# Attention's transfers on SyncE in program order, V in three buffers and asked for sooner, fills and a reciprocal moved later

## The chip, the cores and the metric

The kernel runs on one core of one Trainium2 chip. The metric is the device time of one execution in microseconds (us). A core has five engines that run their own instruction lists in order and wait for each other by semaphores: TensorE (PE, matmuls), VectorE (DVE), ScalarE (ACT), GpSimd (POOL) and SyncE (SP). SP computes nothing here; it issues nearly all of the transfers from memory. ACT and POOL issue a few.

## The reference, cut to what matters

Three layers follow each other. Only the first is touched by the change.

```python
# attention: q, k, v are (2, 12, 448, 64)
scores = cap * tanh(scale * q @ k.T / cap)
attn = exp(scores - max); attn = attn / (sum(attn) + 1e-9)
x = attn @ v                                   # -> (2, 448, 768)
# gated MLP with a spatial gate (w_in, g_ln, w_sg, b_sg, w_out)
h = gelu(x @ w_in); u, v = halves of h
x = x + (u * (w_sg @ layernorm(v) + b_sg)) @ w_out
# gated convolution (w_in, conv_w, w_out)
h = relu(x @ w2_in); out = (h * sigmoid(conv3(h))) @ w2_out
```

## The kernel before

**Attention.** The 24 heads are taken as 12 pairs N. A pair has two rounds R = 2N and 2N + 1 (`half` 0 and 1). In a round PE computes scores (tile `sc`), ACT takes tanh and then exp of them (`raw`, one tanh and one exp for each round), and PE multiplies the `raw` of two rounds earlier with V and with ones (tile `pv`, function `values`). So values of pair N run in rounds 2N + 2 and 2N + 3 (the first pair sooner). There is one PSUM buffer for the scores. In an even round DVE adds two halves of `raw` (`sm`), which a later multiplication with ones sums up.

After a pair's second values ACT copies `pv` to `E`; the next pair's values wait for that copy. For two pairs at a time POOL sends the sums (`ss`) through memory: `s1` in `norm` takes the reciprocal on DVE and writes it out, `s1b` reads it back to all partitions (`rb`), and `s2` multiplies `E` by `rb` on DVE and splits the result into `X`, high part on ACT and low part on DVE. `later(k, fn)` runs a step k ticks later; a round has two ticks, one between scores and values, and one behind the values.

**Fills.** The table `FILL` puts matmuls of the next layer (`mo<-X,WI`) between a round's scores and its values: in three rounds six matmuls each of the first output tile, in two later rounds 18 each of the second and third. They need `X` of finished pairs and pieces of `w_in`. Their PSUM tile `mo` has one buffer, which is free when a gelu in three steps (`g` on ACT, `g` on DVE and ACT, `u` on DVE) has read it.

**Transfers.** `load(n)` asks for q and k of pair n (`qr` with three buffers, `kr` with two), two pairs ahead. `load_v(n)` asks for three quarters of V; the fourth, for all pairs, is `vlast`. `wdec` asks for a piece of `w_in` (`f`, 512 KB, four buffers) in the rounds of `WIN`; ACT or DVE decode it in steps (`hd`, `f`, `WI`). `columns` asks for `g_ln` and `conv_w` in round 1, whose decode steps are 24 columns wide. A scheduler places the instructions of each engine by a simulated timeline of its own; `pin` (`issue_after`) keeps an instruction behind another. SP's transfers carry no pin, so that their order on SP is the scheduler's.

At the start 18 matmuls on the tile `wz` warm PE up while the first q and k come.

**Behind attention** PE runs the other layers' matmuls with no gap to speak of; the change does not alter that part's instructions.

Of the kernel before, what the change touches and what calls it, by code (L numbers as in the profile page):

```python
# [9 lines left out]
F32 = mybir.dt.float32  # L10
F32R = mybir.dt.float32r
U32 = mybir.dt.uint32
U16 = mybir.dt.uint16
# [6 lines left out]
P = 128  # L20
# [13 lines left out]

NFAST = 1

FILL = {13: (0, 0, 2), 17: (0, 2, 4), 21: (0, 4, 6), 23: (1, 0, 6), 25: (2, 0, 6)}

TAKEN = 3

# [11 lines left out]
def stages(  # L52
# [18 lines left out]
    V, A, T, G = nc.vector, nc.scalar, nc.tensor, nc.gpsimd  # L71

    now = [0]
    lasta, lastv, lastr = [None], [None], [None]

    def pin(last):
        return tc.issue_after(last[0].ins) if last[0] is not None else ExitStack()

    due = {}

    def later(k, fn):
        due.setdefault(now[0] + k, []).append(fn)
# [43 lines left out]
    def decode_half(hi, lo, src, pool, bufs, wait, hi_eng, top_eng):  # L126

        n = src.shape[1]
        r = pool.tile([P, 512, 2], U32, tag="f64", name="f64", bufs=bufs)[:, :n]
        words = r.rearrange("p c w -> p (c w)").bitcast(U16)  # L130
        nc.sync.dma_start(words[:, : 4 * n - 1], src.rearrange("r c w -> r (c w)").bitcast(U16)[:, 1:])
        low = r[:, :, 0]
        top = words.rearrange("p (c w) -> p c w", w=4)[:, :, 2].bitcast(BF16)
        heads.append(heads.pop(0))
        hd = heads[-1][:, :n]

        def s1():
            half = hd.bitcast(F16).rearrange("p (c w) -> p c w", w=2)[:, :, 1]
            with pin(lasta), pin(lastv):
                if top_eng == "a":  # L140
                    A.activation(half, top, AF.Copy)
                else:
                    V.tensor_copy(half, top)

        def s2():
            V.scalar_tensor_tensor(
                out=low, in0=low, scalar=13, in1=hd, op0=ALU.logical_shift_right, op1=ALU.bitwise_or
            )
            if hi_eng == "a":
                A.activation(hi, f(low), AF.Copy)  # L150
            else:
                V.tensor_copy(hi, f(low))

        def s3():
            V.tensor_tensor(out=lo, in0=f(low), in1=f(hi), op=ALU.subtract)

        for k, fn in zip(wait, (s1, s2, s3)):
            later(k, fn)

    def decode(hi, lo, src, pool, bufs, wait=(1, 2, 3), hi_eng="a", cols=512, low_eng="v", top_eng="a"):  # L160

        if heads:
            return decode_half(hi, lo, src, pool, bufs, wait, hi_eng, top_eng)
        n = src.shape[1]
        r = pool.tile([P, cols, 2], U32, tag="f64", name="f64", bufs=bufs)[:, :n]
        nc.sync.dma_start(r, src)
        h, l = r[:, :, 1], r[:, :, 0]

        def s1():
            with pin(lasta), pin(lastv):  # L170
                A.activation(f(h), f(h), AF.Copy, scale=2.0**-112)  # L171
                if low_eng == "a":

                    A.activation(l, l, AF.Copy, scale=0.93 * 2.0**-29)  # L174
                else:
                    V.tensor_scalar(
                        out=l, in0=l, scalar1=29, scalar2=None, op0=ALU.logical_shift_right
                    )

        def s2():  # L180
            V.scalar_tensor_tensor(  # L181
                out=l, in0=h, scalar=3, in1=l, op0=ALU.logical_shift_left, op1=ALU.bitwise_or
            )
            V.scalar_tensor_tensor(  # L184
                out=l, in0=h, scalar=0x80000000, in1=l, op0=ALU.bitwise_and, op1=ALU.bitwise_or
            )
            if hi_eng == "a":
                A.activation(hi, f(l), AF.Copy)
            else:
                V.tensor_copy(hi, f(l))  # L190

        def s3():
            V.tensor_tensor(out=lo, in0=f(l), in1=f(hi), op=ALU.subtract)

        for k, fn in zip(wait, (s1, s2, s3)):
            later(k, fn)
# [60 lines left out]
        return eye  # L257

    def columns(pool):
        nc.sync.dma_start(gbc, g_ln.partition_broadcast(P))  # L260
        decode(cw[:, 0], cw[:, 1], conv_w, pool, 4 if bounded else 3)

    def attention(att, psa):
# [10 lines left out]
        def load(n):  # L274
            b, p = divmod(n, NPAIR)
            qr = att.tile([P, S], F32, tag="qr", name="qr", bufs=3)
            kr = kraw[n % 2]
            for h in range(2):
                r = slice(h * D, (h + 1) * D)
                nc.sync.dma_start(qr[r], qT[b, p, r, h])  # L280

            dma = (nc.sync if n else nc.scalar).dma_start
            dma(kr[:D], kT[b, p, :D, 0])
            dma(kr[D:, :ST], kT[b, p, D:, 1, D:])
            dma(kr[D:, ST:], kT[b, p, D:, 1, :D])
            qraw[n] = qr, kr
# [1 line left out]
        vf = {}  # L288

        def load_v(n):  # L290
            vf[n] = att.tile([P, 3, P], F32, tag="V", name="V", bufs=2)
            nc.sync.dma_start(vf[n], vL[divmod(n, NPAIR)][:, :3])

        Qt = {}

# [28 lines left out]
        load_v(0)  # L324
        vlast = att.tile([P, B * NPAIR, P], F32, name="vlast")

        def load_vlast(eng, n0, n1):
            v = vL.rearrange("b n p g c -> p (b n) g c")
            for h in range(2):
                r = slice(h * D, (h + 1) * D)  # L330
                for c in range(2):
                    eng.dma_start(vlast[c * D : (c + 1) * D, n0:n1, r], v[r, n0:n1, 3, r])

        load_vlast(nc.scalar, 0, 3)
        if WARM:

            wz = att.tile([P, S], F32R, name="wz")
            V.memset(f(wz), 0.0)
            wps = psa.tile([P, 4, 512], F32, tag="sc", name="wps", bufs=1)[:, 0, :S]
            for i in range(WARM):  # L340
                T.matmul(wps, lhsT=wz[:, :P], rhs=wz, start=True, stop=True)  # L341
# [140 lines left out]
        def norm(N, both):  # L482
            b, p = divmod(N, NPAIR)
            if N >= B * NPAIR - NFAST:
                return norm_pe(N, both)

            j = N % 2
            last = N == B * NPAIR - NFAST - 1
            m = 1 if last else 2
            if j == 0:  # L490
                pairs[:] = (
                    att.tile([P, 2 * (S + HS)], F32, tag="E", name="E", bufs=3),
                    att.tile([P, 14], F32, tag="ss", name="ss", bufs=2)[:, : 7 * m],
                )
            e, ss = pairs
            A.activation(e[:, j * (S + HS) : (j + 1) * (S + HS)], both, AF.Copy)
            u = j * (2 * S + HS)
            G.dma_start(ss[j * P // m : (j + 1) * P // m], e[::32, u : u + HS])
            if j == 0 and not last:
                return  # L500

            rb = att.tile([P, 2, S], F32, tag="rb", name="rb", bufs=2)
            eb = e[:, HS : HS + m * S].rearrange("p (j c) -> p j c", j=m)
            rb = rb[:, :m]

            ds = []


            def s1():
                with pin(lastv):  # L510
                    V.tensor_scalar(out=ss, in0=ss, scalar1=guard, scalar2=None, op0=ALU.add)
                V.reciprocal(out=ss, in_=ss)
                ds.append(dr.tile([m, 2, 2, HS], F32, tag=f"d{m}", name="d"))
                d = ds[0]
                G.dma_start(d.rearrange("j h f (p c) -> (j h f p) c", c=7 * m), ss)

            def s1b():
                (d,) = ds
                for h in range(2):
                    for i in range(m):  # L520
                        G.dma_start(
                            rb[h * D : (h + 1) * D, i].rearrange("p (f c) -> p f c", f=2),
                            d[i, h].partition_broadcast(D),
                        )

            def s2():
                with pin(lastv):
                    V.tensor_tensor(out=eb, in0=eb, in1=rb, op=ALU.mult)
                with pin(lasta):
                    lastv[0] = split(eb, X[:, 0, p - j : p + 1, b], X[:, 1, p - j : p + 1, b], "a")  # L530

            later(3, s1)
            later(4, s1b)
            later(13, s2)

        def norm_pe(N, both):
# [20 lines left out]
        for R in range(2 * NN + LAGS[1]):  # L557
# [1 line left out]
            if R == 1:  # L559
                columns(att)  # L560
            if R == 4:
                load_vlast(nc.sync, 3, NN)
            for j, at in enumerate(WIN):
                if at == R:
                    top_eng = "v" if R < 11 else "a"
# [1 line left out]
            if R < 2 * NN:  # L567
                if half == 0 and N + 2 < NN:
                    load(N + 2)
                if R == 1:  # L570

                    start_values(0)
# [18 lines left out]
            if R - done >= LAGS[R >= LAGS[2]]:  # L591
                values(*divmod(done, 2))
                done += 1
            if half and N + 1 < NN:
                load_v(N + 1)
            tick()
        for _ in range(9):
            tick()
        assert not due
        heads.clear()  # L600
        lasta[0] = lastv[0] = None

    def exact_attention(att, psa):

# [405 lines left out]
```

## Time and profile before

| what | value |
|---|---|
| median of 3 runs | 350.54 us (350.42 to 351.92) |
| the profiled execution | 351.55 us, its span 349.8 us |
| PE busy | 322.5 us, 92% of the span |
| DVE busy | 239.3 us, 68% |
| ACT busy | 223.8 us, 64% |
| attention | the first 136 us, about |

The span runs from the first to the last instruction of the execution; the time of a run has some 1.75 us around it. Engine shares are means over stages that differ, so the stages are read one by one.

### The profile page before, as it was taken

The numbers are of one execution on the slowest core, as the hardware profiler recorded it, in microseconds if no ns is written. First come the engines' busy times: TensorE is split into PE (matmuls) and PEld (weight loads), VectorE is DVE, ScalarE is ACT, GpSimd is POOL, SyncE is SP. The second block draws the span as 40 slices with busy tenths as digits, with TensorE's granted clock in tenths as the row PEclk, the third lists the DMA queues.
The fourth block names the chain that finished last, engine by engine and source line by source line (L and its number), as shares of the span: only waits on it lengthen the run. The fifth ranks groups of instructions, "written<-read, shape, count | busy, mean of one in ns | idle before, by whom it ended". The sixth has DMA issues, their size and how long they took to land.

```text
span 349.8 us, 6271 instructions
## 1 busy us (share of the span) xinstructions
PE 322.5 (92%) x2380; PEld 263.9 (75%) x2380; DVE 239.3 (68%) x471; ACT 223.8 (64%) x357; POOL 37.7 (11%) x74
## 2 busy tenths in 40 slices
PE   8989289796979899999999999999999999999992
PEld 6456156464645678898889999999999999999992
DVE  4453847628494559999799778999795999990000
ACT  1899629769696835766676555454875789882110
POOL 4000302113130332022111100000000000000000
PEclk9999879989998999999999999999999999999999
DMA  5777665537240113421232357000286022012211
GB/s 139 212 197 238 170 176 161 140 98 197 93 136 25 57 53 118 105 84 44 64 104 74 133 165 278 0 2 0 61 252 231 5 87 88 2 52 110 80 52 34
DMA packets 22062, 37.73 MB, mean 108 GB/s; under 512 B 7320, under 2 KB 14376, under 8 KB 22024
## 3 DMA queue, kind: packets, MB, share of 16 engines
q1 hardware_dynamic: 19320, 34.21, 32.0%
q0 software_dynamic: 1632, 2.61, 2.9%
q10 hardware_dynamic: 1072, 0.43, 0.5%
q8 instruction: 20, 0.33, 0.4%
q14 instruction: 18, 0.15, 0.1%
HBM read 34.40 MB, written 2.79 MB: 106 GB/s over the span
## 4 chain that ended last, share of the span: by engine, by line
PE 79%; ACT 6%; DMA 5%; DVE 4%; SPq 3%; issue 2%; DVEq 0%; ACTq 0%
PE mo L101 17%; PE mo L102 17%; PE mo L103 17%; PE pv L365 8%; PE sc L365 4%; PE mo L365 3%; PE mo L715 3%; PE mo L716 3%; PE mo L717 3%; DMA qr<-in_qT_dram 2%; ACT raw L379 2%; PE wps L341 2%; DMA V<-in_vL_dram 2%; ACT raw L380 2%; DMA kr<-in_kT_dram 1%
## 5 line engine op out<-in xcount | busy, mean ns | idle before, releaser
L101 PE MATMUL mo<-X,WI 128*128 128x448 f32 x126 | 46.1, 367 | 0.3 <-DVE u L220 0.3
L102 PE MATMUL mo<-X,WI 128*128 128x448 f32 x126 | 46.0, 366 | 0.0
L103 PE MATMUL mo<-X,WI 128*128 128x448 f32 x126 | 45.9, 365 | 0.0
L365 PE MATMUL pv<-raw,V 128*32 128x224 f32 x576 | 36.0, 381 | 10.0 <-DMA V<-in_vL_dram 7.9
L379 ACT ACTIVATE raw<-sc 128x1792 f32<-128x1792 f32 (+1 forms) x22 | 32.4, 1471 | 12.8 <-PE sc L365 12.6
L365 PEld LDWEIGHTS pv<-raw,V 128*32 128x32 f32 x576 | 19.7, 115 | 23.5 <-issue 14.6
L380 ACT ACTIVATE raw<-raw 128x1792 f32<-128x1792 f32 (+3 forms) x26 | 36.8, 1413 | 0.8
L102 PE MATMUL mo<-HG,W 128*128 128x448 f32 x96 | 34.8, 365 | 0.0
L103 PE MATMUL mo<-HG,W 128*128 128x448 f32 x96 | 34.7, 365 | 0.0
L101 PE MATMUL mo<-HG,W 128*128 128x448 f32 x96 | 34.1, 365 | 0.0
L365 PE MATMUL sc<-Q,K 64*128 64x448 f32 x216 | 28.7, 387 | 2.3 <-ACT raw L379 2.1
L171 ACT ACTIVATE f<-f 128x256 f32<-128x256 f32 (+2 forms) x44 | 22.7, 516 | 10.3 <-DMA f<-in_w_in_dram 5.9
L365 PEld LDWEIGHTS sc<-Q,K 64*128 64x128 f32 x216 | 18.5, 185 | 12.7 <-ACT raw L379 7.2
L181 DVE SCALAR_TENSOR_TENSOR f<-f 128x256 uint32<-128x256 uint32 (+2 forms) x44 | 22.3, 516 | 8.1 <-ACT f L174 7.9
L101 PEld LDWEIGHTS mo<-X,WI 128*128 128x128 f32 x126 | 23.6, 187 | 2.8 <-DVE u L220 0.8
L102 PEld LDWEIGHTS mo<-X,WI 128*128 128x128 f32 x126 | 23.7, 188 | 2.0
L103 PEld LDWEIGHTS mo<-X,WI 128*128 128x128 f32 x126 | 23.6, 188 | 2.0
L174 ACT ACTIVATE f<-f 128x256 uint32<-128x256 uint32 (+2 forms) x44 | 22.6, 513 | 0.0
L184 DVE SCALAR_TENSOR_TENSOR f<-f 128x256 uint32<-128x256 uint32 (+2 forms) x44 | 22.4, 515 | 0.1
L895 ACT ACTIVATE o<-mo 128x448 f32<-128x448 f32 x12 | 6.3, 540 | 24.9 <-PE mo L103 21.3
L428 DVE TENSOR_TENSOR sm<-raw 128x896 f32<-128x896 f32 x12 | 13.0, 1085 | 11.1 <-ACT raw L380 9.7
L365 PE MATMUL mo<-X,WI 128*128 128x448 f32 x54 | 13.4, 388 | 6.8 <-DVE X L98 4.1
(148 smaller groups left out, 700.8 us busy)
## 6 DMA issues: line engine op xcount, KB each, us to landing
f<-in_w_in_dram SPq DMA_DIRECT2D x12, 512.0 KB, 5.7
f<-in_w_out_dram SPq DMA_DIRECT2D x24, 256.0 KB, 4.6
f<-in_w_in_dram SPq DMA_DIRECT2D x12, 511.8 KB, 4.6
f<-in_w_out_dram SPq DMA_DIRECT2D x8, 384.0 KB, 3.1
qr<-in_qT_dram SPq DMA_DIRECT2D x24, 112.0 KB, 3.0
out_dram<-o SPq DMA_DIRECT2D x12, 224.0 KB, 1.9
rb<-d POOLq DMA_DIRECT2D x22, 112.0 KB, 3.6
V<-in_vL_dram SPq DMA_DIRECT2D x12, 192.0 KB, 3.0
```

The costliest lines, as they stand in the source:

```text
L101: matmul(ps, lhsT=whi, rhs=xhi, start=start, stop=False)
L102: matmul(ps, lhsT=whi, rhs=xlo, start=False, stop=False)
L103: matmul(ps, lhsT=wlo, rhs=xhi, start=False, stop=stop)
L171: A.activation(f(h), f(h), AF.Copy, scale=2.0**-112)
L174: A.activation(l, l, AF.Copy, scale=0.93 * 2.0**-29)
L181: V.scalar_tensor_tensor(out=l, in0=h, scalar=3, in1=l, op0=ALU.logical_shift_left, op1=ALU.bitwise_or)
L184: V.scalar_tensor_tensor(out=l, in0=h, scalar=0x80000000, in1=l, op0=ALU.bitwise_and, op1=ALU.bitwise_or)
L365: lastm[0] = T.matmul(*args, **kw)
L379: A.activation(x, ps, AF.Tanh, **sc)
L380: lasta[0] = A.activation(x, x, AF.Exp, scale=creg)
L428: V.tensor_tensor(out=held[N], in0=raw[:, 0:2], in1=raw[:, 2:4], op=ALU.add)
L715: T.matmul(ps, lhsT=xs(0, k), rhs=WI[1][:, 0, k], start=k == 0, stop=False)
```

## The change

Six things change, all in attention: every transfer that SP issues there goes through `sync`, which pins it behind the one before, so SP keeps the program's order; `V` has three buffers instead of two; `load_v(N + 1)` moves from the end of round 2N + 1 to round 2N, behind `load(N + 2)`; the first part of `vlast` moves from ACT's queue to SP's; `s1` and `s1b` of `norm` come one tick later; and the three small fills move from rounds 13, 17 and 21 to 14, 18 and 22. The warm-up tile `wz` takes a buffer of the tag `rb`.

```diff
-FILL = {13: (0, 0, 2), 17: (0, 2, 4), 21: (0, 4, 6), 23: (1, 0, 6), 25: (2, 0, 6)}
+FILL = {14: (0, 0, 2), 18: (0, 2, 4), 22: (0, 4, 6), 23: (1, 0, 6), 25: (2, 0, 6)}
...
+    def sync(dst, src):
+
+        if lasts:
+            with pin(lasts):
+                lasts[0] = nc.sync.dma_start(dst, src)
+        else:
+            nc.sync.dma_start(dst, src)
...
-        nc.sync.dma_start(r, src)
+        sync(r, src)
...
-                nc.sync.dma_start(qr[r], qT[b, p, r, h])
-
-            dma = (nc.sync if n else nc.scalar).dma_start
+                sync(qr[r], qT[b, p, r, h])
+
+            dma = sync if n else nc.scalar.dma_start
...
-            vf[n] = att.tile([P, 3, P], F32, tag="V", name="V", bufs=2)
-            nc.sync.dma_start(vf[n], vL[divmod(n, NPAIR)][:, :3])
+            vf[n] = att.tile([P, 3, P], F32, tag="V", name="V", bufs=3)
+            sync(vf[n], vL[divmod(n, NPAIR)][:, :3])
...
-        load_vlast(nc.scalar, 0, 3)
+        load_vlast(0, 3)
...
-            wz = att.tile([P, S], F32R, name="wz")
+            wz = att.tile([P, S], F32R, tag="rb", name="wz", bufs=2)
...
-            later(3, s1)
-            later(4, s1b)
+            later(4, s1)
+            later(5, s1b)
             later(13, s2)
...
                 if half == 0 and N + 2 < NN:
                     load(N + 2)
+                if half == 0 and N + 1 < NN:
+                    load_v(N + 1)
...
-            if half and N + 1 < NN:
-                load_v(N + 1)
```

How it moves instructions, at three places. On SP before, from k of pair 5 on (a number behind a name tells one buffer's use from another; `V_421` is V of pair 3, `qr_424` and the `kr0` around it are q and k of pair 6, `kr1` is k of odd pairs):

```order
L283 DMA kr1_90<-in_kT_dram 64x448
L284 DMA kr1_90<-in_kT_dram 64x384
L285 DMA kr1_90<-in_kT_dram 64x64
L939 TENSOR_LOAD one_72
L939 ISA x2
L131 DMA f64_722<-in_w_in_dram 128x2047
L284 DMA kr0_89<-in_kT_dram 64x384
L280 DMA qr_424<-in_qT_dram 64x448 x2
L283 DMA kr0_89<-in_kT_dram 64x448
L285 DMA kr0_89<-in_kT_dram 64x64
L131 DMA f64_827<-in_w_in_dram 128x2047
L292 DMA V_421<-in_vL_dram 128x384
```

On SP in the changed kernel, where V of pair 3 is `V_335` and `qr_329` and `kr0` ahead of it are q and k of pair 4:

```order
L83 DMA V_256<-in_vL_dram 128x384
L83 DMA f64_309<-in_w_in_dram 128x2047
L83 DMA vlast_108<-in_vL_dram 64x9x64 x4
L83 DMA qr_329<-in_qT_dram 64x448 x2
L83 DMA kr0_89<-in_kT_dram 64x448
L83 DMA kr0_89<-in_kT_dram 64x384
L83 DMA kr0_89<-in_kT_dram 64x64
L83 DMA V_335<-in_vL_dram 128x384
L83 DMA f64_382<-in_w_in_dram 128x2047
L83 DMA qr_424<-in_qT_dram 64x448 x2
L83 DMA kr1_90<-in_kT_dram 64x448
```

V of pair 3 stood behind the loads of pairs 5 and 6 and now stands behind those of pair 4, with one piece of w_in between its round's loads and the next.

On PE before, in round 13 (its scores, the first fill, its values):

```order
L365 MATMUL sc<-Q,K_87 128x2x224 x6
L365 MATMUL sc<-qr,kl_91 64x224 x4
L365 MATMUL mo<-X,WI_76 128x448 x6
L365 MATMUL pv<-raw,vlast 64x224 x4
L365 MATMUL pv<-raw,V 32x224 x8
```

And on PE in the changed kernel, in round 14 (its scores, the first fill, its values, the scores of round 15):

```order
L373 MATMUL sc<-Q,K_88 128x448 x12
L373 MATMUL mo<-X,WI_76 128x448 x6
L373 MATMUL pv<-raw,V 32x224 x16
L373 MATMUL pv<-sm,ones_152 32x224 x4
L373 MATMUL sc<-Q,K_88 128x2x224 x6
```

The six matmuls on `mo` moved from behind round 13's scores to behind round 14's; the two other small fills moved in the same way.

On ACT before, around the gelu of the first output tile (fill done in round 21; `g_1219` is that gelu, 1792 columns of `raw` are an even round, 1344 an odd one):

```order
L379 ACTIVATE raw<-sc 128x1344
L380 ACTIVATE raw<-raw 128x1344
L213 ACTIVATE g_1219<-mo 128x448
L217 ACTIVATE g_1219<-g_1219 128x448
L141 ACTIVATE hd_141<-f_1145 128x512
L496 ACTIVATE E<-pv 128x672
L379 ACTIVATE raw<-sc 128x1792
L380 ACTIVATE raw<-raw 128x1792
```

And on ACT in the changed kernel, where the fill is done in round 22 and `g_1265` is that gelu:

```order
L149 ACTIVATE hd_141<-f_1141 128x512
L504 ACTIVATE E<-pv 128x672
L387 ACTIVATE raw<-sc 128x1792
L221 ACTIVATE g_1265<-mo 128x448
L388 ACTIVATE raw<-raw 128x1792
L225 ACTIVATE g_1265<-g_1265 128x448
L149 ACTIVATE hd_141<-f_1199 128x512
L387 ACTIVATE raw<-sc 128x1344
```

The exp of the round now stands between the gelu's two steps on ACT.

## Rows read from the trace of the kernel before

**Rows 1.** Busy time by stretch (attention, the rest); columns named in the first line.

```profile
core 0: us, PE busy (x) PEld busy (x) DVE busy (x) ACT busy (x) POOL busy (x), PEclk, DMA share, GB/s
0.00:136.00 136.00, 115.12 (x1376) 75.50 (x1377) 78.43 (x154) 95.15 (x88) 27.17 (x61) 0.95 0.50 142
136.00:350.00 214.00, 207.40 (x1006) 188.40 (x1004) 160.92 (x318) 128.66 (x269) 10.53 (x14) 1.00 0.27 86
```

**Rows 2.** PE's waits, first 140 us: us in total, times, longest.

```profile
PE pv L365 <- DMA V<-in_vL_dram: 7.9, 1, 7.9
```

**Rows 3.** Timeline of PE, 35 to 60 us: start, us, operation, [idle before <-releaser].

```profile
35.97 1.48 PE L365 MATMUL sc<-Q,K 64*128 64x448 f32 x12
45.32 3.08 PE L365 MATMUL pv<-raw,V 128*32 128x224 f32 x32 [7.87 <-DMA V<-in_vL_dram]
...
48.71 0.88 PE L365 MATMUL sc<-Q,K 64*128 64x448 f32 x6
...
52.11 1.49 PE L365 MATMUL sc<-Q,K 64*128 64x448 f32 x12
53.53 1.76 PE L365 MATMUL pv<-raw,V 128*32 128x224 f32 x32
...
55.59 0.88 PE L365 MATMUL sc<-Q,K 64*128 64x448 f32 x6
...
56.83 0.56 PE L365 MATMUL pv<-raw,vlast 64*64 64x224 f32 x8
...
58.99 1.50 PE L365 MATMUL sc<-Q,K 64*128 64x448 f32 x12
```

**Rows 4.** Busy time and granted clock (PEclk), 46 to 48 us, columns as in rows 1.

```profile
46.00:48.00 2.00, 2.00 (x28) 1.27 (x24) 0.00 (x0) 0.00 (x0) 0.00 (x0) 0.50 1.10 253
```

**Rows 5.** Timeline of SP's queue, first 40 us.

```profile
11.05 0.42 SPq L131 DMA_DIRECT2D f<-in_conv_w_dram  x1
...
17.50 2.70 SPq L332 DMA_DIRECT2D vlast<-in_vL_dram  x4
...
34.58 0.48 SPq L284 DMA_DIRECT2D kr<-in_kT_dram  x1
```

**Rows 6.** The chain that ended last, 0 to 60 us: start, us, what.

```profile
39.07 6.12 DMA V<-in_vL_dram
```

**Rows 7.** Timeline of PE, 63 to 123 us.

```profile
63.30 0.61 PE L365 MATMUL sc<-qr,kl 64*64 64x224 f32 x8
...
66.94 1.28 PE L365 MATMUL mo<-X,WI 128*128 128x448 f32 x5 [1.65 <-DVE X L98]
68.15 0.65 PE L365 MATMUL pv<-raw,vlast 64*64 64x224 f32 x8
...
71.89 1.53 PE L365 MATMUL sc<-Q,K 64*128 64x448 f32 x12
...
115.12 3.93 PE L365 MATMUL mo<-X,WI 128*128 128x448 f32 x18
...
122.23 1.76 PE L365 MATMUL pv<-raw,V 128*32 128x224 f32 x32 [0.97 <-ACT E L496]
```

**Rows 8.** Timeline of ACT, 15 to 89 us.

```profile
15.91 0.21 ACT L141 ACTIVATE hd<-f 128x24 f16<-128x24 bf16 x1
...
79.45 0.77 ACT L141 ACTIVATE hd<-f 128x512 f16<-128x512 bf16 x1
80.09 0.69 ACT L496 ACTIVATE E<-pv 128x672 f32<-128x672 f32 x1
...
83.98 0.93 ACT L97 ACTIVATE X<-E 128x896 fp32r<-128x896 f32 x1
...
86.75 1.33 ACT L380 ACTIVATE raw<-raw 128x1344 f32<-128x1344 f32 x1
```

**Rows 9.** DMA issues: tensor, queue, operation, count, KB each, median us to landing.

```profile
kr<-in_kT_dram SPq DMA_DIRECT2D x11, 16.0 KB, 2.9
```

**Rows 10.** Timeline of all engines, 106 to 110 us.

```profile
106.94 0.55 ACT L213 ACTIVATE g<-mo 128x448 f32<-128x448 f32 x1 [0.43 <-PE mo L365]
...
108.78 0.62 DVE L220 SCALAR_TENSOR_TENSOR u<-g,mo 128x448 f32<-128x448 f32 x1 [0.64 <-ACT g L217]
```

More of the change, by code (lines that the diff above doesn't have):

```diff
@@ L73, in stages @@
     now = [0]
-    lasta, lastv, lastr = [None], [None], [None]
+    lasta, lastv, lastr, lasts = [None], [None], [None], [None]
     def pin(last):
         return tc.issue_after(last[0].ins) if last[0] is not None else ExitStack()
+    def sync(dst, src):
[4 more added lines that the diff above has]
+            nc.sync.dma_start(dst, src)
     due = {}
@@ L130, in decode_half @@
         words = r.rearrange("p c w -> p (c w)").bitcast(U16)
-        nc.sync.dma_start(words[:, : 4 * n - 1], src.rearrange("r c w -> r (c w)").bitcast(U16)[:, 1:])
+        sync(words[:, : 4 * n - 1], src.rearrange("r c w -> r (c w)").bitcast(U16)[:, 1:])
         low = r[:, :, 0]
@@ L259, in columns @@
     def columns(pool):
-        nc.sync.dma_start(gbc, g_ln.partition_broadcast(P))
+        sync(gbc, g_ln.partition_broadcast(P))
         decode(cw[:, 0], cw[:, 1], conv_w, pool, 4 if bounded else 3)
@@ L325, in attention, with load_vlast @@
         vlast = att.tile([P, B * NPAIR, P], F32, name="vlast")
-        def load_vlast(eng, n0, n1):
+        def load_vlast(n0, n1):
             v = vL.rearrange("b n p g c -> p (b n) g c")
@@ L331, in load_vlast @@
                 for c in range(2):
-                    eng.dma_start(vlast[c * D : (c + 1) * D, n0:n1, r], v[r, n0:n1, 3, r])
-        load_vlast(nc.scalar, 0, 3)
+                    sync(vlast[c * D : (c + 1) * D, n0:n1, r], v[r, n0:n1, 3, r])
+        load_vlast(0, 3)
         if WARM:
-            wz = att.tile([P, S], F32R, name="wz")
+            wz = att.tile([P, S], F32R, tag="rb", name="wz", bufs=2)
             V.memset(f(wz), 0.0)
@@ L561, in attention @@
             if R == 4:
-                load_vlast(nc.sync, 3, NN)
+                load_vlast(3, NN)
             for j, at in enumerate(WIN):
@@ L601, in attention @@
         lasta[0] = lastv[0] = None
+        lasts.clear()
     def exact_attention(att, psa):
```

## The prediction

> **What bounds the kernel now.** I read the busy table by stretch first. From 136 us to the end TensorE (PE) is busy 207.4 of 214 us, and its list of waits holds nothing there; before 136 us it is busy only 115.1 of 136 [rows 1]. All that can be won lies in the attention stage. The list of PE's waits there [rows 2] gives the largest, 7.9 us for one V tile; the next are for X, the finished pairs, ahead of the fills. What these cost is read from PE's timeline, start to start, since a wait also empties the pipeline and can lower the clock.
>
> An undisturbed pair of heads is the yardstick: scores of pair 5 start at 52.11, of pair 6 at 58.99, so a pair takes 6.88 us; in it the first scores take 53.53 - 52.11 = 1.42, then values and the second scores 56.83 - 53.53 = 3.30 [rows 3].
>
> *The V stall.* Scores of pair 4 start at 35.97 and the values behind them at 45.32 instead of 37.39: 7.93 us lost. These values then run to 48.71, 3.39 us where the same piece takes 55.59 - 53.53 = 2.06: 1.33 more, because the granted clock is at half (0.50 over 46 to 48 us, 1.2 instead of 2.4 GHz) after the idle time [rows 3, 4]. Together **9.26 us**. Why V was late: the queue of SyncE (SP) issued a piece of kr only at 34.58 [rows 5], and the chain shows V asked for at 39.07 and landed 6.12 later [rows 6]. By SP's order this V, of pair 3, stands behind q and k of pair 6 and behind two pieces of w_in.
>
> *The fill stalls.* The six matmuls of a fill in round 13 begin after the scores at 63.30; the next values start at 68.15, and the next scores at 71.89 [rows 7]. From 58.99 to the values at 122.23 (less their own wait of 0.97) there are 62.27 us. Work in it: six pairs, 41.28; the large fill of 18, 3.93; three fills of six, a third of that each, 3.93; together 49.14. So **13.13 us** are lost around the three small fills and the waits on ScalarE (ACT) beside them. In the first, the values from 68.15 to 71.89 take 3.74 us where the same piece takes 58.99 - 56.83 = 2.16, the sign of the lower clock again.
>
> **The change, part by part.**
>
> *V sooner, SP in program order.* V of pair 3 is now requested in round 4 (scores of pair 2), behind one w_in piece instead of behind the loads of pair 6. With three buffers it needs only the values of pair 0, long done. It is used in round 8, so the request leads by two pairs, 13.8 us less the queue's own issues; the landing of V that stalled was 6.12 [rows 6]. For the later pairs V waits for values that end in the round just before the request; again nearly two pairs of lead. I count the whole 9.26 as gained. Queued behind V on SP are one w_in piece and the next q and k: they are asked for a round or more ahead of their use and are not due at once (priced as a rival below). The part of vlast that leaves ACT's queue gives ACT nothing: its first tanh waits for PE's first scores, and these for the warm-up.
>
> *Cost at the start.* The four vlast requests now stand on SP ahead of q and k of pair 2, then V of pair 1, and only then conv_w. Four vlast requests took 2.70 us [rows 5], so conv_w, issued at 11.05, moves to about 13.8, or 14.3 with half a microsecond for V. Its decode on ACT stands right ahead of the tanh of round 2, and ran at 15.91 without a wait [rows 8], so conv_w takes at most 15.91 - 11.47 = 4.4 us to land. At the nearest small transfer, 2.9 us for 16 KB of kr [rows 9], it lands at 14.3 + 0.4 + 2.9 = 17.6. K of pair 2 moves as well, and VectorE (DVE) prepares it ahead of conv_w's second step. The gaps in which SP waited ahead of 11.05 take up part of the shift; with half a microsecond of it there, the tanh starts 1.2 us late. ACT's chain of tanh and exp then sets round 4's scores, so this is lost for good. Bounds: 0 (the gaps take up all) and 17.6 - 15.91 + 1.5 = 3.2 (the longest landing). I take **-1.2**.
>
> *Fills a round later.* A fill in round 14 stands behind the first scores of pair 7, one round (3.4 us) later on PE, while X comes on ACT and DVE where it came before. In the first stall PE restarts at 66.94, released by DVE's X [rows 7], 7.95 us after round 12's start at 58.99. The moved fill is reached one pair and 1.42 us after that start, at 8.30: just behind X. So the X waits and the half clock go. The margin is thin (0.35 us), but ACT's own lateness moves PE, not X.
>
> What comes in their place is ACT. A pair on ACT without gaps, from the decode step at 79.45 to the end of the exp at 88.08, is 8.63 us, with two decode steps (0.64 each to the start of the next), one X step of 0.93 and no gap in its 8 instructions [rows 8]; bare, 6.42. Rounds 16 to 19 hold three decode steps and one X: 12.84 + 0.93 + 1.92 = 15.69 against 2 x 6.88 + 1.31 = 15.07 for PE. That is 0.6 of wait; in the other two blocks the totals fit, but E, the copy out of PSUM that values wait for, comes late in each where X or a decode step sits ahead. The 0.97 at 122.23 [rows 7] is such a wait. I take 0.6 for each of three blocks, **1.8**; bounds 0 and 3 x 0.97 = 2.9.
>
> *The large fill meets the small one.* Both use one PSUM buffer, freed when DVE has made u. Before, the last small fill was in round 21 and the large in 23; now 22 and 23. Between them lie values and second scores, 3.30 us. The chain took from g at 106.94 to the end of u at 109.40, 2.5 us right behind the fill [rows 10]. In the new order ACT has an exp of 1792 columns between its two steps (estimated 1.7 from the 1.33 of the 1344-column one [rows 8]), DVE has the sum of raw, which waits for that exp, ahead of u, and the round's tanh stands ahead of g; I allow 0.5 for each of these two: 5.2. New stall **1.9**; bounds 0.9 (exp alone: 4.2 - 3.3) and 1.9 + 1.6, if the clock falls too, as it cost 3.74 - 2.16 = 1.58 in the first fill [rows 7].
>
> *Reciprocal a step later.* Half a round, 1.7 us, on a chain that starts four rounds ahead of X; cover is those rounds. Without it, X and the fills would come up to 1.7 us later each. I take 0. The warm-up tile in rb's buffers is free long before rb's first use: 0.
>
> **Sum.** 9.26 - 1.2 + (13.13 - 1.8 - 1.9 = 9.43) = 17.5 us. The profiled execution took 351.55 (span 349.8), so 334.1; it lies 1.0 above the median of the runs, 350.54, which gives 333.0. I forecast **333.0 us**. A measurement of this kernel tells about 0.5% from no change.
>
> **Rivals.**
>
> (a) *X is late anyway*, because the fill is reached only 0.35 us after X and X moves with ACT: the three stalls stay, and only V's 9.26 less 1.2 is won: 342.5. For it: DVE holds K, Q and the sum ahead of X. Against: it did so in the measured 7.95 too. 0.12, with the mirror case (V still late, fills cured, 342) in it.
>
> (b) *ACT and the shared buffer cost nothing*: 9.26 + 13.13 - 0 to 1.2: 328 to 330. 0.10.
>
> (c) *The slower side: SP's queue blocks.* A V request at the head waits for PE's values, and q and k behind it for V. K's request ends about 0.8 us into its pair's first round; DVE has it ahead of a sum that the next pair's values use at 6.88 + 1.42 + 1.65 = 9.95 (1.65 is 32 of 40 matmuls of 2.06), and I allow 1.1 for that sum. So it hurts from a landing of 8 us on, and eats the gain of 17.5 only from about 10 us on each of nine pairs. kr's small piece lands in 2.9 [rows 9]. The rule that speaks for this is in the Trainium skill, "DMA: Bandwidth & Descriptors", section "Anatomy of one DMA — SWDGE (gpsimd) path": a transfer's semaphore wait is served on the issuing sequencer, ahead of dispatch, so one held request holds all behind it. The trace agrees (kr at 34.58 holds V back). By that rule alone a queue in program order could be slower than the scheduler's; above 352, 0.04.
>
> (d) *Clock and start at their bad ends*: 333 + 1.6 + 2.0 and up to 2 from ACT: 336 to 339. 0.06.
>
> (e) The order moves and PE still waits for something else as long: within 0.5%, 0.02. My own case, 331 to 336, has 0.66.
>
> Range 329 to 338.5 (0.80: mine, (d) and most of (b)). Faster 0.93, same 0.03, slower 0.04.
>
> **What would show it.** V: no PE wait for V over 1 us, and PE's clock at full over what is now 44 to 50 us. Fills: the first fill right behind 12 score matmuls without a DVE or ACT wait. Start: round 2's tanh at about 18 us behind a wait for conv_w. Shared buffer: one PE wait of some 2 us for u ahead of the fill of 18. Attention ends some 17.5 us sooner, the rest stays at 214 us. Wrong if values still wait for V or X, or if DVE waits for kr in every pair.

## The result, and the profile after

The changed kernel took **334.92 us** (median of 4 runs, 333.77 to 337.11) against 351.13 for the kernel before, run beside it: ratio 0.9545, 95% interval 0.9485 to 0.9605. The forecast was 333.0, range 329 to 338.5. The gain is 16.2 us where 17.5 was forecast. The profiled execution was the longest of the four, 337.11 with a span of 335.3, 14.4 us below the profiled one before.

Attention's last matmuls (`pv<-E,sel`), before and after:

```profile
134.68 0.98 PE L547 MATMUL pv<-E,sel 128*64 128x224 f32 x8
120.34 0.98 PE L555 MATMUL pv<-E,sel 128*64 128x224 f32 x8
```

Attention ends 14.3 us sooner, at 121.3 us instead of 135.7. The rest is what it was: the busy time by stretch of the kernel after, cut at 119 us and so some 2 us ahead of attention's end, has PE busy 210.04 of the last 217 us [rows 1].

```profile
core 0: us, PE busy (x) PEld busy (x) DVE busy (x) ACT busy (x) POOL busy (x), PEclk, DMA share, GB/s
0.00:119.00 119.00, 108.48 (x1360) 72.56 (x1361) 75.40 (x151) 93.82 (x87) 26.81 (x60) 0.97 0.58 157
119.00:336.00 217.00, 210.04 (x1021) 190.21 (x1020) 162.90 (x321) 129.34 (x270) 10.79 (x14) 0.99 0.27 88
```

PE's waits in the first 125 us, kernel after (us in total, times, longest):

```profile
PE pv L373 <- ACT E L504: 3.3, 3, 1.8
PE sc L373 <- ACT raw L387: 3.3, 4, 2.1
...
PE mo L373 <- DVE u L228: 1.4, 1, 1.4
```

V and X are gone. They headed this list before, V with 7.9 [rows 2], X with these:

```profile
PE mo L365 <- DVE X L98: 4.1, 3, 1.6
PE mo L365 <- ACT X L97: 2.7, 3, 1.2
```

What is left is ScalarE and the gelu's `u`. Where the time came from is read start to start on PE's timeline of the kernel after:

```profile
22.24 2.61 PE L373 MATMUL sc<-Q,K 64*128 64x448 f32 x12 [2.11 <-ACT raw L387]
24.77 3.23 PE L373 MATMUL pv<-raw,V 128*32 128x224 f32 x32
...
31.98 1.49 PE L373 MATMUL sc<-Q,K 64*128 64x448 f32 x12
...
38.87 1.49 PE L373 MATMUL sc<-Q,K 64*128 64x448 f32 x12
40.28 1.76 PE L373 MATMUL pv<-raw,V 128*32 128x224 f32 x32
...
52.62 1.49 PE L373 MATMUL sc<-Q,K 64*128 64x448 f32 x12
...
59.62 1.49 PE L373 MATMUL sc<-Q,K 64*128 64x448 f32 x12
61.05 1.50 PE L373 MATMUL mo<-X,WI 128*128 128x448 f32 x6
62.47 1.76 PE L373 MATMUL pv<-raw,V 128*32 128x224 f32 x32
...
69.98 1.76 PE L373 MATMUL pv<-raw,V 128*32 128x224 f32 x32 [0.55 <-ACT E L504]
...
76.05 1.49 PE L373 MATMUL sc<-Q,K 64*128 64x448 f32 x12 [0.54 <-ACT raw L387]
...
87.64 1.76 PE L373 MATMUL pv<-raw,V 128*32 128x224 f32 x32 [1.79 <-ACT E L504]
...
100.77 3.94 PE L373 MATMUL mo<-X,WI 128*128 128x448 f32 x18 [1.36 <-DVE u L228]
...
107.90 1.76 PE L373 MATMUL pv<-raw,V 128*32 128x224 f32 x32 [0.97 <-ACT E L504]
```

Scores of pair 4 (38.87) are followed by their values at 40.28 without a wait; from there to pair 6 (52.62) two pairs take 13.75 us instead of 23.02 [rows 3]. The first fill (61.05) stands right behind the scores, and its values follow it directly. From pair 6 to the values of round 24 it is now 55.28 us (107.90 - 52.62) instead of 63.24.

One piece went the other way. Rounds 4 to 6 take 9.74 us (31.98 - 22.24), where a pair takes 6.88: the score matmuls take 2.61 and the values 3.23 instead of 1.49 and 1.76. The windows of the kernel after say why:

```profile
22.00:24.00 2.00, 1.76 (x10) 1.59 (x12) 1.37 (x5) 1.50 (x2) 0.00 (x0) 0.50 1.17 232
24.00:26.00 2.00, 2.00 (x22) 0.99 (x19) 1.93 (x4) 1.11 (x1) 0.00 (x0) 0.50 1.28 197
```

The granted clock is 0.50, 1.2 GHz, behind PE's wait of 2.11 us for ACT. In the profile before, a wait of 1.74 at the same place was followed by full clock:

```profile
22.21 1.48 PE L365 MATMUL sc<-Q,K 64*128 64x448 f32 x12 [1.74 <-ACT raw L379]
```

At the start, ACT's rows after show what conv_w costs there:

```profile
16.38 0.23 ACT L149 ACTIVATE hd<-f 128x24 f16<-128x24 bf16 x1 [1.11 <-DMA f<-in_conv_w_dram]
...
17.00 1.65 ACT L387 ACTIVATE raw<-sc 128x1792 f32<-128x1792 f32 x1
```

### The profile page after: what moved, and what is told of

The parts are those of the page before. It is cut to its first block, busy times and chain, and to the rows that moved or that the text cites. A ratio compares the mean times of both kernels' runs of the same rounds, so it can differ in the third digit from the quotient of the medians.

```text
span 335.3 us, 6265 instructions
## 1 busy us (share of the span) xinstructions
PE 318.5 (95%) x2380; PEld 262.8 (78%) x2380; DVE 238.3 (71%) x471; ACT 223.2 (67%) x357; POOL 37.6 (11%) x74
## 3 DMA queue, kind: packets, MB, share of 16 engines
q0 software_dynamic: 1632, 2.61, 3.1%
## 4 chain that ended last, share of the span: by engine, by line
PE 79%; ACT 10%; DMA 4%; SPq 2%; issue 2%; DVE 1%; ACTq 0%; DVEq 0%
PE mo L109 18%; PE mo L110 18%; PE mo L111 18%; PE pv L373 8%; PE sc L373 6%; ACT raw L387 4%; PE mo L724 3%; PE mo L726 3%; PE mo L725 3%; SPq L83 2%; ACT raw L388 2%; PE mo L373 2%; DMA qr<-in_qT_dram 1%; ACT hd L149 1%; DMA f<-in_conv_w_dram 1%
## 5 line engine op out<-in xcount | busy, mean ns | idle before, releaser
L109 PE MATMUL mo<-X,WI 128*128 128x448 f32 x126 | 46.0, 367 | 0.3 <-DVE u L228 0.3
L110 PE MATMUL mo<-X,WI 128*128 128x448 f32 x126 | 46.0, 366 | 0.0
L111 PE MATMUL mo<-X,WI 128*128 128x448 f32 x126 | 45.9, 365 | 0.0
L373 PE MATMUL pv<-raw,V 128*32 128x224 f32 x576 | 34.6, 370 | 3.5 <-ACT E L504 3.3
L373 PE MATMUL sc<-Q,K 64*128 64x448 f32 x216 | 29.9, 399 | 3.8 <-ACT raw L387 3.3
L110 PEld LDWEIGHTS mo<-HG,W 128*128 128x128 f32 x96 | 18.0, 188 | 1.4
L109 PEld LDWEIGHTS mo<-HG,W 128*128 128x128 f32 x96 | 18.0, 188 | 1.4
```

Of the source, the lines that this page charges most:

```text
L109: matmul(ps, lhsT=whi, rhs=xhi, start=start, stop=False)
L110: matmul(ps, lhsT=whi, rhs=xlo, start=False, stop=False)
L111: matmul(ps, lhsT=wlo, rhs=xhi, start=False, stop=stop)
L373: lastm[0] = T.matmul(*args, **kw)
```

## The experiments

In each comparison the ratio goes with the kernel before, run on the same chip (medians 350.01, 349.54 and 351.11 in the three groups); medians are of 6 or 12 runs. No kernel leaves any of the work out. To compare profiles, attention is cut into stretches, from PE's starts (us): S, from the first scores to the scores of round 4; A, from those to the scores of round 12, undisturbed 4 x 6.88 = 27.52; B, from there to the values of round 24, where the work is 49.14; R, from there to the span's end.

| kernel | S | A | B | R | span | median |
|---|---|---|---|---|---|---|
| before | 14.22 | 36.78 | 63.24 | 227.6 | 349.8 | 351.13 |
| before2 | 14.66 | 36.48 | 64.56 | 227.2 | 349.8 | 351.56 (one run) |
| before3 | 14.40 | 35.38 | 64.37 | 227.5 | 349.2 | 351.01 (one run) |
| after | 15.07 | 30.38 | 55.28 | 227.4 | 335.3 | 334.92 |
| after2 | 14.93 | 27.53 | 54.38 | 227.7 | 331.7 | 336.01 |
| v_only | 15.91 | 30.28 | 63.24 | 227.2 | 343.8 | 345.62 |
| fill_only | 14.65 | 34.28 | 53.96 | 227.5 | 337.5 | 341.23 |
| pin_only | 14.23 | 29.14 | 67.77 | 227.4 | 346.1 | 348.27 |
| v_nopin | 16.51 | 29.96 | 66.08 | 227.4 | 347.2 | 347.16 |
| warm3 | 16.15 | 27.53 | 54.60 | 227.4 | 333.0 | 335.10 |
| conv_first | 14.53 | 29.06 | 55.98 | 227.3 | 334.3 | 334.44 |
| e_first | 14.23 | 27.53 | 54.67 | 227.8 | 332.4 | 335.72 |
| s1_late | 15.65 | 29.06 | 55.67 | 227.3 | 335.5 | 335.43 |
| combo | 14.23 | 27.51 | 56.40 | 227.5 | 333.4 | 334.32 |

R is the same in all fourteen within 0.6 us, so what was won or lost stands in attention. (The first scores start between 6.94 and 8.19 us, which is no difference of the kernels: the warm-up matmuls ahead of them take 5.3 to 6.8 us.)

### The change in parts

**v_only**, the changed kernel with these lines as before (it keeps vlast's move and the new place of `wz`):

```diff
+FILL = {13: (0, 0, 2), 17: (0, 2, 4), 21: (0, 4, 6), 23: (1, 0, 6), 25: (2, 0, 6)}
+            later(3, s1)
+            later(4, s1b)
```

> The V part of the change alone (SP in program order, three V buffers, V asked for two rounds sooner); fills and the reciprocal step as in the kernel before. Theory A (the two gains add): 9.3 us for V less 0 to 1.2 at the start, so 8 to 9.3 us below the kernel before, 341.5 to 342.8 us; no PE wait for V over 1 us, but the three waits for X ahead of the fills stay, the first at about 56 us instead of 64. Theory B (the gains overlap: with V in time the fills come early and their stalls grow by what V gave): less than 4 us below the kernel before. Theory C (V in program order cures the X waits as well): 15 us or more below it, and the fills alone give nothing.

Measured: 345.62 us, ratio 0.9858 (0.9804 to 0.9911). PE's waits of v_only:

```profile
PE mo L373 <- DVE X L106: 4.1, 3, 1.7
PE sc L373 <- ACT raw L387: 3.6, 3, 2.1
PE mo L373 <- ACT X L105: 2.7, 3, 1.1
```

No wait for V, and the three for X as they were; B is 63.24, as in before (64.56 and 64.37 in its two other profiles). So neither B nor C holds, but theory A's size is short by 3.6 to 4.9 us: 8 to 9.3 was expected, and the medians differ by 4.4. The profile has it: S is 1.5 us longer than the 14.43 of before (mean of its three profiles), since conv_w held ACT for 1.95 us, and behind round 4 the clock fell, 2.76 us in A. With the mean stall of the three profiles of before (8.7, below), 8.7 - 1.5 - 2.8 is 4.4. That one profile fits the medians so well is in part luck: the ratio's 1.4% is 5.0 us, and the span lies 5.8 below the mean of before's three.

**fill_only**, the kernel before with the new FILL, and s1, s1b still at 3 and 4:

```diff
-FILL = {13: (0, 0, 2), 17: (0, 2, 4), 21: (0, 4, 6), 23: (1, 0, 6), 25: (2, 0, 6)}
+FILL = {14: (0, 0, 2), 18: (0, 2, 4), 22: (0, 4, 6), 23: (1, 0, 6), 25: (2, 0, 6)}
```

> The fills a round later and the reciprocal a step later alone; SP's order, the V buffers and the time of V's request as in the kernel before. Theory A (the gains add): 8 to 9.4 us below the kernel before, 341 to 342.5 us, with PE's wait of about 7.9 us for V still there and no wait for X ahead of the first fill. Theory B (the gains overlap, the V stall had already given X time): less than 4 us below. Theory C (without the new V order nothing is won here): within 1 us of the kernel before.

Measured: 341.23 us, ratio 0.976 (0.9705 to 0.9815). The expectation speaks of the reciprocal too, but this kernel left it where it was before, and its fills found X in time all the same: no wait for X is left, B is 53.96. Theory A holds. V still stalls, for less:

```profile
37.04 1.49 PE L365 MATMUL sc<-Q,K 64*128 64x448 f32 x12
42.06 2.69 PE L365 MATMUL pv<-raw,V 128*32 128x224 f32 x32 [3.54 <-ACT raw L380]
```

The profile puts the wait down to ACT, whose exp was long done; SP issued this V only at 36.61. The two parts give 1.4% and 2.4%, together 3.8%; the whole gave 4.55% in its first comparison and 3.6% in the second (after2). They add within the intervals.

**pin_only** (the order alone) and **v_nopin** (buffer and sooner request alone), both v_only with a piece taken back:

```diff
 pin_only
-            vf[n] = att.tile([P, 3, P], F32, tag="V", name="V", bufs=3)
+            vf[n] = att.tile([P, 3, P], F32, tag="V", name="V", bufs=2)
-                if half == 0 and N + 1 < NN:
-                    load_v(N + 1)
...
+            if half and N + 1 < NN:
+                load_v(N + 1)
 v_nopin
-        if lasts:
-            with pin(lasts):
-                lasts[0] = nc.sync.dma_start(dst, src)
-        else:
-            nc.sync.dma_start(dst, src)
+        nc.sync.dma_start(dst, src)
```

> SP in program order alone: two V buffers and V asked for at the end of a pair's second round, as before; fills as before. Compared with the run of the V part whole. Theory A (V was late because it stood behind the loads of a later pair; the program's order alone puts it ahead of them): the wait for V is gone or under 1 us, the time is within 1 us of the V part whole. Theory D (the third buffer and the sooner request are what counts): V still waits for 3 us or more in some rounds, and the time is 4 us or more above the V part whole.

> Three V buffers and the sooner request alone, with SP's order left to the scheduler; fills as before. Theory A (the sooner request alone is enough as well, since V needs only a buffer that is long free): the wait for V gone or under 1 us, within 1 us of the V part whole. Theory E (the order is what counts: the scheduler puts V behind other transfers again): a V wait of 3 us or more and 4 us or more above the V part whole. If both this and the order alone cure V, either edit would have done.

Measured: 348.27 us, ratio 0.994 (0.9904 to 0.9976), and 347.16, ratio 0.9931 (0.989 to 0.9972). Neither has a wait for V, so each edit by itself cures the stall; D and E fall. But both are 1.5 to 2.7 us slower in the median than the V part whole, at the edge of the intervals, which A did not expect. It is not V: the fills' stretch B grew to 67.77 and 66.08. In pin_only PE waits longer for the low part of X, and the clock falls behind it (60 to 64 us at 0.50 to 0.70):

```profile
60.46 1.98 PE L373 MATMUL mo<-X,WI 128*128 128x448 f32 x5 [2.85 <-DVE X L106]
```

X is late there because SP's queue blocks. With two buffers and V asked for at the end of a pair, a V request at the head of the queue waits until PE's values have freed a buffer, and q, k and w_in stand behind it. Of the waits of SP's queue and of DVE in pin_only, 20 to 125 us:

```profile
SPq L83 <- PE pv L373: 48.0, 9, 12.6
```

```profile
DVE hd L151 <- DMA f<-in_w_in_dram: 5.9, 3, 3.0
DVE K L103 <- DMA kr<-in_kT_dram: 3.1, 3, 1.7
```

From 50.57, when a late piece of w_in has come, DVE works without a gap up to the scaling of E for X at 55.02. In v_only, with the third buffer and the sooner request, the first is 12.6 us, DVE waits 1.1 us for w_in and never for kr, and its longest wait for X is that of before (1.7). So the order alone cures V but brings in what the prediction feared as rival (c), and the other two edits keep that away. In v_nopin the order is the scheduler's again, and DVE waits 3.3 us for a q as in the kernel before. One profile each doesn't say how much of the loss is this and how much the clock, which fell in three places of B in pin_only and in two in v_only and v_nopin.

### Why the kernel before loses a different amount each time

> The kernel before once more, for a second profile. The medians of the changed kernel and of its V part gain less than the profiles' 18 and 9.3 us would give. Theory J (the stall for V differs from execution to execution, since SP is let go by VectorE, which waits for a piece of q behind pieces of w_in; the profile shown had a long one): PE's loss from round 8 to round 10, 9.26 us in the profile shown, is 3 to 8 us here while the stalls of the fills are as they were. Rival K (the stall is always the same, the rest varies): it is 9 to 9.5 us.

> A third profile of the kernel before, for the same question: theory J has the loss from round 8 to round 10 anywhere from 3 to 10 us, different from the other two by over 1 us; rival K 9 to 9.5 us. What the clock does behind round 4 is read here too: theory G (chance) has a fall to half over about 22 to 28 us in some profiles of this kernel as well, at 2.9 us each.

The two more profiles of the kernel before took 351.56 and 351.01 us. Stretch A exceeds 27.52 by 9.26, 8.96 and 7.86, on average 8.7. So the stall varies, by 1.4 us here, and K does not hold, though before2's 8.96 lies outside the 3 to 8 that J named and near K's. In fill_only, whose SP order up to this V is the same, V cost 5.2 (pair 4 to pair 5 in 12.09 us, 49.13 - 37.04, less 6.88); but there the clock had fallen behind round 4, so PE itself came 1.5 us later to this V. J's root of the stall is seen in the rows: one landing. DVE's rows for Q of the next pair and for the `kr` behind it, in before, and for Q in before3:

```profile
33.63 0.45 DVE L304 TENSOR_SCALAR Q<-qr,one 128x448 fp32r<-128x448 f32 x1 [5.11 <-DMA qr<-in_qT_dram]
34.00 0.55 DVE L98 TENSOR_TENSOR K<-kr,K 128x384 fp32r<-128x384 f32 x1
```

```profile
31.82 0.45 DVE L304 TENSOR_SCALAR Q<-qr,one 128x448 fp32r<-128x448 f32 x1 [3.56 <-DMA qr<-in_qT_dram]
```

DVE stands until that q has landed; then it reads `kr`, which frees the buffer that the request at the head of SP waits for (34.58 in before, 32.77 in before3, 32.85 in fill_only), and V is asked for 3.8 to 4.9 us behind that. SP's rows of before show where the q was asked for:

```profile
22.70 1.54 SPq L131 DMA_DIRECT2D f<-in_w_in_dram  x3
24.33 1.47 SPq L280 DMA_DIRECT2D qr<-in_qT_dram  x2
```

It stands just behind three pieces of w_in and takes 33.63 - 24.33 = 9.3 us. The Trainium skill, "DMA: Bandwidth & Descriptors", section "Two DMAs through the same engine are not ordered", says that descriptors in one queue of a DMA engine start in order; the trace agrees, a small transfer pays for the large ones ahead of it. But this landing accounts for only a part of what varies. From its request to its use q takes 9.3, 8.9 and 8.7 us in the three profiles; V's own landing takes 6.1, 5.2 and 5.5, and the half clock behind the stall costs 1.3, 2.5 and 1.9. In the changed kernel one piece of w_in goes out per pair, and DVE's waits for q in attention sum to 0.3 us. No clock fall behind round 4 was seen in the three profiles of before.

### The clock behind round 4

**after2** is the changed kernel again; **warm3** keeps PE busy where it waits:

```diff
+                if R == 3:
+                    for _ in range(10):
+                        ordered(idle, lhsT=wz[:, :P], rhs=wz, start=True, stop=True)
```

> The changed kernel once more, for its times beside the next three on one chip and for a second profile. Theory F (the fall of PE's clock behind round 4's wait is part of the change: PE has waited over 2 us for ACT there because the tanh of round 2 came late behind conv_w): 334 to 336 us, and the clock is at half over about 22 to 28 us in this profile too. Theory G (the fall is chance): 333 to 336 us, and with some luck no fall in this profile.

> The changed kernel with ten idle matmuls of 448 columns behind the scores of round 3, so that PE is busy where it waits about 2.1 us for ACT's exp ahead of round 4's scores. Theory F (the wait lowers the clock): granted clock 1.00 from 20 to 30 us, scores of round 4 to scores of round 6 take 6.9 us instead of 9.7, and the time is 2 to 3 us below the changed kernel's. Theory G (the fall has another cause, or hardly ever happens): the clock falls all the same or the time stays within 1 us of the changed kernel's.

Measured: 336.01 us (333.48 to 336.53), ratio 0.9636 (0.9582 to 0.9691), and 335.10, ratio 0.9617 (0.9561 to 0.9673). PE's timeline of after2:

```profile
22.12 1.48 PE L373 MATMUL sc<-Q,K 64*128 64x448 f32 x12 [2.11 <-ACT raw L387]
...
28.99 1.50 PE L373 MATMUL sc<-Q,K 64*128 64x448 f32 x12
...
49.65 1.49 PE L373 MATMUL sc<-Q,K 64*128 64x448 f32 x12
...
104.03 1.76 PE L373 MATMUL pv<-raw,V 128*32 128x224 f32 x32 [0.97 <-ACT E L504]
```

The same program, the same wait of 2.11 us, and no fall: rounds 4 to 6 take 6.87, the windows show 1.00 throughout attention, A is 27.53, and the span is 331.7. So the fall is not in every execution, as theory F has it. Over all profiles with a wait of 1.7 to 2.1 us there (all but warm3's), the clock fell in seven (after, v_only, fill_only, pin_only, v_nopin, conv_first, s1_late; 1.5 to 2.9 us each) and not in six. The Trainium skill, "TensorE: Matmul & The Clock Gate", section "What's actually happening", says that the activity monitor runs free of the kernel, which such a mixture agrees with. But it isn't rare. Each run has a mean granted clock on record. In the profiles of the changed kernel and of the edits on it that have the new fills, it is 0.994 or 0.995 where no fall was seen in attention (after2, e_first, warm3) and 0.985 to 0.993 where one was (after, conv_first, combo, s1_late). Of the changed kernel's ten runs two have 0.995 and take 333.5 and 333.8 us; the other eight have 0.985 to 0.992 and take up to 337.1. Which wait each of them fell behind, the mean doesn't tell.

Without the wait, warm3 had no fall in its profile either, and four of its six runs have 0.995 to 0.998. PE's rows of warm3:

```profile
21.18 2.33 PE L373 MATMUL idle<-wz 128*128 128x448 f32 x10
23.43 1.49 PE L373 MATMUL sc<-Q,K 64*128 64x448 f32 x12
```

The idle matmuls cost nothing: from the tanh of round 2 (18.13) to these scores it takes 5.30 us, in after2 5.23 (22.12 - 16.89). That S is longer is conv_w, which held ACT for 2.22 us here. That leans toward theory F, with the wait as what makes a fall likelier, but six runs against ten are few. In the medians nothing is won that the intervals could tell, and how often the clock falls behind just this wait, and what it costs on average, stays open.

### The start, and the waits for ScalarE

```diff
 conv_first
-                if half == 0 and N + 1 < NN:
+                if half == 0 and 0 < N and N + 1 < NN:
                     load_v(N + 1)
+                if R == 1:
+                    load_v(1)
 e_first
-            A.activation(e[:, j * (S + HS) : (j + 1) * (S + HS)], both, AF.Copy)
+            lasta[0] = A.activation(e[:, j * (S + HS) : (j + 1) * (S + HS)], both, AF.Copy)
 s1_late
-            later(4, s1)
-            later(5, s1b)
+            later(7, s1)
+            later(8, s1b)
```

> The changed kernel with the request of pair 1's V put behind that of conv_w on SP; nothing else is moved. Theory A (conv_w behind V on the queue is what holds ACT's step ahead of the tanh of round 2): ACT's wait for conv_w falls from 1.11 us to 0.3 or less, round 4's scores start 0.8 us or more sooner after the first scores than the 15.07 us of the changed kernel, time 0.5 to 1.5 us lower (more if PE's shorter wait ahead of round 4 also saves the clock). Rival (the four vlast requests ahead do it, or the landing itself varies): the wait stays at about 1 us and so does the time.

Measured: 334.44 us, ratio 0.9587 (0.9529 to 0.9645), 0.7 to 1.6 us below the three others run on its chip, less than the intervals can tell. ACT's wait for conv_w is 0.58 in its profile and 0.20 in combo, which has the same edit; with V ahead it is 1.11, 0.96, 1.95, 2.22, 1.76 and 0.24 in the six kernels that have SP's new order (after, after2, v_only, warm3, s1_late, e_first), 0 in the three of before. In v_nopin, where the scheduler put V there too, it is 2.56. The value of 0.24 is of the execution whose first scores came latest (8.19), so that ACT was late by itself. S is 0.54 us shorter than after's (A asked for 0.8). pin_only, with vlast ahead of conv_w and V behind it, waits 0.19. So A has the direction: with V ahead the wait is mostly about 1 to 2.6 us, with V behind it 0.6 or less. Its size varies too much for one profile.

> The changed kernel with the copy E held to ACT's written order, so that a w_in decode step no longer stands between the copy's inputs and E: on ACT that step moves behind E in five places. Theory H (values wait for E because ACT stands in that step, which itself waits for a buffer that DVE frees late): PE's longest wait for E goes from 1.79 to 0.6 us or less, time 1 to 1.5 us lower. Theory I (ACT has simply too much to do in those rounds): the waits move to the tanh or the exp behind E, and the time stays within 0.5 us.

Measured: 335.72 us, ratio 0.9641 (0.9582 to 0.9701). PE's waits of e_first:

```profile
PE sc L373 <- ACT raw L387: 4.2, 5, 1.7
...
PE pv L373 <- ACT E L504: 0.8, 1, 0.8
```

E went from 3.3 (2.4 in after2) to 0.8, and `raw` from 3.3 to 4.2; the time is after2's within 0.3 us. That is theory I: the waits moved behind E. ACT still stands in the decode step, for the buffer that DVE frees late:

```profile
83.70 0.80 ACT L149 ACTIVATE hd<-f 128x512 f16<-128x512 bf16 x1 [0.70 <-DVE f L154]
```

> The changed kernel with the scaling of the sums and their reciprocal three steps later still, so that on VectorE they no longer stand, waiting for their transfer, ahead of the sum of raw and of the decode step whose buffer ScalarE needs next. Theory L (this wait of VectorE is the root of the longest wait of values for E): no PE wait for E over 1 us, waits for E and raw from round 12 on 1 to 2 us less in sum, time 1 to 2 us below the changed kernel's 334.9 to 336.0. Theory M (X and so the fills come late instead, since their chain starts later): a wait for X of 0.5 us or more at one or more fills, time the same or up to 3 us higher.

> Three edits on the changed kernel together: V of pair 1 behind conv_w on SP, E in ScalarE's written order, the sums' scaling three steps later. If each gives what the profiles show of its wait (0.9 at the start, 0.8 to 1.5 for E, 0.5 to 1 for raw), the time is 332 to 334 us; if the waits only change places, 334.5 to 336 us, and PE's waits for ScalarE and VectorE from round 12 on sum to 4 us or more, as in the changed kernel.

Measured: s1_late 335.43 us, ratio 0.9626 (0.9557 to 0.9695); combo, all three edits, 334.32, ratio 0.9622 (0.9557 to 0.9687). In s1_late the longest wait for E is 0.97, as L said, but one for raw of 1.47 and one for X of 0.49 came, and the time did not move. The one for X speaks for M only weakly, since conv_first, without this edit, has one of 0.48 too. In combo the price is plain. DVE's row and PE's, of combo:

```profile
69.85 1.09 DVE L536 TENSOR_TENSOR E<-E,rb 128x896 f32<-128x896 f32 x1 [4.48 <-DMA rb<-d]
```

```profile
73.78 1.74 PE L373 MATMUL sc<-Q,K 64*128 64x448 f32 x12 [1.99 <-ACT raw L387]
```

The later reciprocal makes `rb` late; DVE waits 4.48 us for it, ACT behind it for X, PE 1.99 us for ACT, and the clock falls (0.50 over 76 to 78 us). B, 56.40, is 2.0 us longer than after2's, and eats what S gave (0.7). PE's waits for ACT and DVE from round 12 on sum to 4.6 us, against 5.2 in after and 4.4 in after2: they changed places, as the second case of the expectation has it, though the time is 0.2 us below its 334.5. The medians of combo and conv_first are the lowest, but no kernel here is shown to beat the changed one. Two things were not run: a second `hd` buffer does not fit in the core's memory, and the reciprocal back at its old steps gives the same order of instructions on every engine as the changed kernel, so there is nothing to time.

## Why the prediction was right

The bound, the places and the mechanisms were right; the total came out 1.9 us above the forecast. That it came so close is in part luck: V was priced by the longest of three stalls, and the fall of the clock behind round 4 was not in the sum. By terms, against the profile of before:

- *V*, forecast 9.26: two pairs from 38.87 take 13.75 instead of 23.02, **9.27**. V of pair 3 goes out at 26.03 and is used at 40.28. The runs added two things. The order alone or the sooner request alone would have cured the wait for V, though each alone came out 1.5 to 2.7 us slower than both, at the edge of the intervals. And the 9.26 is the high end: three profiles of before have 8.7 on average. The queue was held by q's landing behind w_in, one step ahead of the kr that the prediction named.
- *Fills*, forecast 13.13 - 1.8 - 1.9 = 9.43: **7.96** in the profile of after, 8.86 in after2, 9.3 to 10.6 in fill_only against the three of before. The first fill has no wait. The shared buffer cost 1.36 (forecast 1.9). The mis-sized term is ACT: its two waits for E and one for raw from round 12 to round 20 sum to 0.55 + 0.54 + 1.79 = 2.88 (after2: 2.05), forecast 1.8. The prediction counted ACT's work; the 1.79 is not work but a chain, in DVE's rows and ACT's of the kernel after:

```profile
84.15 0.23 DVE L519 TENSOR_SCALAR ss<-ss,one 128x14 f32<-128x14 f32 x1 [4.29 <-DMA ss<-E]
...
85.52 0.68 DVE L154 SCALAR_TENSOR_TENSOR f<-f,hd 128x512 uint32<-128x512 uint32 x1
```

```profile
86.23 0.78 ACT L149 ACTIVATE hd<-f 128x512 f16<-128x512 bf16 x1 [1.13 <-DMA V<-in_vL_dram]
86.88 0.70 ACT L504 ACTIVATE E<-pv 128x672 f32<-128x672 f32 x1
```

  On DVE the scaling of the sums waits 4.29 us for its transfer, the decode step stands behind it, and ACT's `hd` waits for that step, which frees the one `hd` buffer at 86.2 (the row names a V that was long there). The wait for E varies with that transfer: fill_only has the same order on ACT and DVE from round 12 on, a wait of 2.51 for the sums there, 0.55 for E, and 1.62 for the three waits together, inside the forecast's 1.8. The remaining 0.9 us of the stretch are small gaps that were not broken down.
- *Start*, forecast -1.2: conv_w's wait is there, 1.11, but the tanh of round 2 starts at 17.00 instead of 16.96, since this execution's first scores came 0.82 sooner. Counted from the first scores, S is 15.32 on average in the six profiles with this order on SP, against 14.43 in three of before: **-0.9**, from +0.2 to -1.7.
- *Reciprocal*, forecast 0: right, as a step later leaves every engine's order as it was, and fill_only's fills are on time without it; three steps further it costs (combo).
- *Not foreseen*: the fall of the clock behind round 4, 2.86 us in the profile of after, none in after2. The prediction priced a fall only at the shared buffer (rival d), where none came.

The sum for the profile: 9.27 + 7.96 - 2.86 with the rest nearly level is 14.4, what the two executions differ by. Without the fall, after2's span is 18.1 below, 0.6 from the 17.5. Rival (a), X late anyway, is refuted by the first fill, though the margin is thin, as forecast: conv_first waits 0.48 us for X at its second. Rival (b), ACT and buffer free, is refuted by the waits for E and u; (c), a blocking queue, by DVE's 0.3 us of waiting for q and the absence of any wait for V. That (c) is no idle fear is shown by pin_only, where the queue stands 48.0 us for PE's values. SP does stand longest for PE's scores (21.5 us in attention), but nobody waits for what is behind it.

## What to carry to other kernels

When a late transfer stalls the compute engine, follow the request back through the queue until something else than the queue is late: here a small q behind three large weight pieces held an engine, which held a buffer, which held the queue. Price a stall that hangs on one landing as a range from several profiles, since one profile may show its high end, as here (9.3, 9.0 and 7.9 us). Cure the next stall in the row together with the first, give requests in program order the buffers and the lead that keep the head of the queue from standing, and don't expect a wait for a busy engine to go away by reordering that engine: it changed places three times here.

## What the runs showed that was not expected

A pause of the same length at the same place of the same program (2.11 us) was followed by TensorE's half clock in one execution and not in another, and one of 1.73 us by it in fill_only but by none of 1.73 in before3; it cost 1.5 to 2.9 us. The 18 warm-up matmuls took from 5.3 to 6.8 us. Runs of one kernel spread over 2 to 6 us on one chip, those of the kernel before over up to 9.5. The shorter runs have the higher mean clock (from 333.5 us at 0.995 to 337.1 at 0.985 in the changed kernel); how much is the falls and how much the start was not separated.
